# A backward decode kernel bound by its DMA: all loads moved to the stores' ring, zeros in longer rows and smaller portions

## The chip, the cores and the metric

The kernel runs on one core of a Trainium2 chip. The metric is the device time of one execution in microseconds; the time given for a kernel is the median of its executions. A profiled execution also has a span, which is some 2 us shorter (300.1 for 301.83 us before the change). A run is called slow when it lies more than 1.5% above the fastest run of the same kernel; ratios use fast runs alone.

The engines have the profile's names: PE multiplies matrices (PEld loads its weights), ACT and DVE compute and copy, Pool computes masks here, SP only issues transfers. A *ring* is the queue in which the transfers that one engine issued wait for the 16 DMA engines; a transfer *lands* when all of it has arrived. Idle DMA is time in which DMA engines have no packet to move.

## The reference

The reference runs one decode step of an attention layer (4 sequences, 32 query heads, 8 K/V heads, the last 1024 of 4096 cached positions) beside a GeGLU feed-forward layer, and returns the output and all gradients:

```python
q = (xn @ wq).reshape(B, Sq, Hq, Dh)                    # B 4, Sq 1, D 512, Hq 32, Dh 128
k = jnp.repeat(k_cache[:, :, Sk - W:, :], rep, axis=1)  # W 1024 of Sk 4096, rep 4
v = jnp.repeat(v_cache[:, :, Sk - W:, :], rep, axis=1)
p = softmax(einsum("bhqd,bhkd->bhqk", q, k) * Dh ** -0.5)
a = einsum("bhqk,bhkd->bhqd", p, v).reshape(B, Sq, Hq * Dh) @ wo
f = (gelu(xn @ w_gate) * (xn @ w_up)) @ w_down          # F 1792
out = x + a + f                                         # xn = layernorm(x)
_out, _vjp = jax.vjp(_f, x, k_cache, v_cache, wq, wo, w_gate, w_up, w_down)
return (_out, *_vjp(grad_out))
```

The gradients of both caches are full-size, 33.6 MB each. Three quarters of each are zeros, since only 1024 positions take part. Writing 50.3 MB of zeros is the largest single piece of traffic.

## The kernel before

It works in four attention blocks (two K/V heads each) after the feed-forward part. Loads are issued by SP, the stores of computed gradients by Pool, the zeros by ACT: three rings on the same 16 DMA engines. Computed gradients pass through three output buffers (`osb`) and four staging buffers (`stg`).

```python
wres = ctx.enter_context(tc.tile_pool(name="wres", bufs=2))    # wo, wq of two blocks
kvp = ctx.enter_context(tc.tile_pool(name="kvp", bufs=3))      # K and V blocks, 1 MB each
outp = ctx.enter_context(tc.tile_pool(name="outp", bufs=3))    # osb_d, osb_g, osb_o, osb_q
...
def load_kv(t, k, g):
    d_, src, nm = ((k_t, A_k_cache, "kb"), (v_t, A_v_cache, "vb"))[k]
    tl = kvp.tile([P, B, J, Dh], BF16, name=nm, tag=nm)
    nc.sync.dma_start(out=tl[:].rearrange("p b j d -> p b (j d)"), in_=...)
...
ZG = 4                                                         # one transfer: 4 heads, 3.15 MB
def zeros(n):
    zsrc = bass.AP(tensor=ztile.tensor, offset=ztile.offset, ap=[list(ztile[:].ap[0]), [0, ZG], [1, ZW]])
    for _ in range(min(n, len(zlist))):
        og, b, g = zlist.pop(0)
        z = store(nc.scalar, og[b, g:g + ZG, 0:K0, :].rearrange("g (m j) d -> m g (j d)", m=P), zsrc, ...)
        if last_act:                                           # keeps its place in ACT's order
            tc.add_manual_dep(z.ins, last_act[-1].ins.name, NoSync)
...
def scores(t, k):
    for g in range(GP):
        for b in range(B):
            ...
            tick(2)                                            # two pieces of deferred gradient work
            if b == 1 and (g, k) != (0, 0):
                zeros(1)                                       # three per block
...
def piece_o(g, i, held):
    if i == 0:
        held["osb"] = outp.tile([P, rep, D], BF16, name="osb_o", tag="o")
    ...
    if i == rep - 1:
        store(nc.gpsimd, out=out_5[...], in_=held["osb"][:], ...)
...
for t in range(NT):
    scores(t, 0); softmax(t); dvdk(t, 0); scores(t, 1); softmax_d(t); dvdk(t, 1)
    odq(t, 0); pre(t + 1); odq(t, 1); fin(t)
    load_next(t)                                               # K/V of t+1 and t+2, weights of t+2
    dw(t)
tick(len(bg))
zeros(len(zlist))                                              # four transfers are left: 12.6 MB
```

## Time and profile before

| | before |
|---|---|
| time | 302.49 us (301.24 to 303.51, three runs) |
| span of the profile | 300.1 us |
| moved | 112.38 MB, of it 50.46 zeros, 30.81 loads, 30.67 stores |
| end of PE's work | 267 us |
| granted PE clock | 0.83 |

The page's slices, its queue table, the windows and the chain are shown and read in the prediction.

### The profile page before, as it was taken

What the parts mean: (1) busy time and instruction counts of PE and PEld (TensorE: products, weight loads), DVE (VectorE), ACT (ScalarE), POOL (GpSimd) and SP (SyncE); (2) the same over time, 40 slices, a digit from 0 to 9 for tenths busy, and PEclk for the clock granted to TensorE, in tenths of its full rate; (3) what the DMA queues carried; (4) which work ended last, traced back from release to release, by engine and by line L of the source; (5) the groups of instructions that cost most, each with busy time, mean ns of one, the idle gap of its engine ahead of it and who ended that gap; (6) DMA issues with size and microseconds to landing.
All of it is one profiled execution on the core that took longest, in us unless ns stands there. A gap on an engine that the chain in (4) does not pass through costs nothing.

```text
span 300.1 us, 6816 instructions
## 1 busy us (share of the span) xinstructions
PE 206.4 (69%) x2956; PEld 141.9 (47%) x2956; DVE 145.1 (48%) x310; ACT 114.4 (38%) x217; POOL 66.4 (22%) x84
## 2 busy tenths in 40 slices
PE   1397987959779986668997876995759779720000
PEld 0396875636447645435764644673436455320000
DVE  6372763544635673364566445564344537760000
ACT  3002645734425554243565243445235417710000
POOL 6000121622032423103513302251032031400000
PEclk9985999887978897997799789799777968955555
DMA  4999999399999999999999999999699995999997
GB/s 137 381 387 382 379 399 403 131 393 398 400 396 331 381 415 416 419 418 424 410 387 409 423 416 419 419 414 408 260 386 359 392 403 211 340 370 407 418 417 322
DMA packets 34149, 112.38 MB, mean 374 GB/s; under 512 B 1408, under 2 KB 7560, under 8 KB 34120
## 3 DMA queue, kind: packets, MB, share of 16 engines
q10 hardware_dynamic: 8580, 50.46, 41.3%
q1 hardware_dynamic: 17732, 30.81, 28.1%
q0 software_dynamic: 7808, 30.67, 26.2%
q8 instruction: 23, 0.38, 0.5%
q14 instruction: 6, 0.05, 0.0%
HBM read 30.93 MB, written 81.01 MB: 373 GB/s over the span
## 4 chain that ended last, share of the span: by engine, by line
PE 49%; DMA 23%; DVE 11%; ACT 3%; issue 3%; SPq 0%; DVEq 0%; ACTq 0%; POOLq 0%
DMA out_dram<-osb_o 11%; PE T_ps L316 10%; PE kv_ps L424 7%; DMA kb<-in_A_k_cache_dram 6%; PE S_ps L321 4%; DMA wd_sb<-in_B_w_down_dram 4%; DVE T_sb L94 3%; PE wqT_ps L488 3%; DMA out_dram<-osb_d 3%; PE woT_ps L268 3%; PE od_ps L396 2%; PE wgT_ps L636 2%; PE acc_ps L168 2%; PE dwg_ps L609 2%; PE wdT_ps L524 2%
## 5 line engine op out<-in xcount | busy, mean ns | idle before, releaser
L94 DVE COPY T_sb<-T_ps 128x1024 bf16<-128x1024 bf16 x64 | 44.2, 691 | 40.5 <-PE T_ps L316 40.1
L92 ACT CAST stg_dv<-kv_ps 128x512 bf16<-128x512 f32 x52 | 28.9, 588 | 39.9 <-PE kv_ps L424 39.5
L92 ACT CAST stg_dk<-kv_ps 128x512 bf16<-128x512 f32 x46 | 25.0, 588 | 15.1 <-PE kv_ps L424 14.9
L316 PE MATMUL T_ps<-ident,kb 128*128 128x128 bf16 x256 | 24.7, 228 | 5.8 <-DMA kb<-in_A_k_cache_dram 5.3
L316 PE MATMUL T_ps<-ident,vb 128*128 128x128 bf16 x256 | 26.4, 252 | 1.4 <-DVE osb_q L94 1.4
L316 PEld LDWEIGHTS <-kb 128*128 128x128 bf16 x256 | 18.5, 102 | 17.0 <-DMA kb<-in_A_k_cache_dram 5.8
L424 PE MATMUL kv_ps<-domr,P_q 128*128 128x512 bf16 x64 | 24.1, 441 | 0.0
L316 PEld LDWEIGHTS <-vb 128*128 128x128 bf16 x256 | 20.2, 114 | 7.6 <-issue 3.7
L92 ACT CAST osb_q<-dwq_ps 128x512 bf16<-128x512 f32 x25 | 13.6, 589 | 21.1 <-DMA out_dram<-osb_o 11.2
L424 PE MATMUL kv_ps<-qmr,dS_q 128*128 128x512 bf16 x64 | 20.8, 410 | 0.6 <-ACT stg_dv L92 0.3
L92 ACT CAST osb_g<-dwg_ps 128x384 bf16<-128x384 f32 (+1 forms) x30 | 14.5, 534 | 13.5 <-PE dwg_ps L609 7.8
L94 DVE COPY woT<-woT_ps 128x1024 bf16<-128x1024 bf16 x16 | 11.1, 692 | 16.1 <-PE woT_ps L268 16.1
L92 ACT CAST osb_o<-dwo_ps 128x512 bf16<-128x512 f32 x23 | 12.9, 587 | 11.5 <-PE dwo_ps L443 10.9
L332 POOL TENSOR_TENSOR dS_q<-dS_b,qmsk 128x1024 bf16<-128x1024 bf16 x4 | 7.5, 1884 | 33.3 <-DVE dS_b L385 33.3
L458 PE MATMUL dwq_ps<-od_r,xnm 128*128 128x256 bf16 x64 | 12.5, 320 | 2.5 <-DVE osb_q L94 2.3
L321 PE MATMUL S_ps<-T_sb,dom 128*32 128x256 bf16 x128 | 10.2, 307 | 5.2 <-DVE T_sb L94 5.2
L94 DVE COPY wqT<-wqT_ps 128x1024 bf16<-128x1024 bf16 x16 | 11.0, 689 | 5.6 <-PE wqT_ps L488 5.4
L488 PEld LDWEIGHTS <-wq_sb 128*128 128x128 bf16 x128 | 11.1, 121 | 5.1 <-issue 4.1
L488 PE MATMUL wqT_ps<-ident,wq_sb 128*128 128x128 bf16 x128 | 13.0, 260 | 0.0
L94 DVE CAST stg_dk<-kv_ps 128x512 bf16<-128x512 f32 x18 | 12.1, 686 | 1.4 <-PE kv_ps L424 1.3
L268 PE MATMUL woT_ps<-ident,wo_sb 128*128 128x128 bf16 x128 | 12.3, 240 | 0.5 <-DVE dST L94 0.3
L98 POOL DMA_DIRECT2D out_dram<-stg_dv x8 | 6.2, 775 | 28.5 <-ACT stg_dv L92 22.8
(187 smaller groups left out, 365.1 us busy)
## 6 DMA issues: line engine op xcount, KB each, us to landing
out_dram<-ztile ACTq DMA_DIRECT2D x16, 3072.0 KB, 16.3
kb<-in_A_k_cache_dram SPq DMA_DIRECT2D x8, 1024.0 KB, 17.4
vb<-in_A_v_cache_dram SPq DMA_DIRECT2D x8, 1024.0 KB, 21.2
out_dram<-stg_dv POOLq DMA_DIRECT2D x8, 1024.0 KB, 10.2
out_dram<-stg_dk POOLq DMA_DIRECT2D x8, 1024.0 KB, 9.4
wo_sb<-in_A_wo_dram SPq DMA_DIRECT2D x4, 1024.0 KB, 17.0
wq_sb<-in_A_wq_dram SPq DMA_DIRECT2D x4, 1024.0 KB, 18.1
out_dram<-osb_o POOLq DMA_DIRECT2D x8, 512.0 KB, 11.8
```

The lines of the kernel that those rows point to most:

```text
L92: last_act.append(nc.scalar.copy(out=out, in_=in_))
L94: return nc.vector.tensor_copy(out=out, in_=in_)
L98: d = eng.dma_start(out=out, in_=in_)
L168: nc.tensor.matmul(ps[:, c, :], lhsT=lf(c), rhs=rhs, start=(k == 0), stop=(k == len(terms) - 1))
L268: nc.tensor.transpose(wT_ps[:, i, c, :], wo_sb[:, 2 * h2 + i, c * P:(c + 1) * P], ident[:])
L316: nc.tensor.transpose(T_ps[:, j, :], blks[(t, g)][:, b, j, :], ident[:])
L321: nc.tensor.matmul(ps[q * RG:(q + 1) * RG, :], lhsT=lf[:, s * RG:(s + 1) * RG], rhs=T_sb[:, q * WQ:(q + 1) * WQ], start=(g == 0 and b == 0 ...
L332: nc.gpsimd.tensor_tensor(out=dst[:], in0=src[:].unsqueeze(1).broadcast_to([P, NQ, WQ]), in1=qmsk[:].unsqueeze(2).broadcast_to([P, NQ, WQ] ...
L396: nc.tensor.matmul(od_ps[b * RB:b * RB + rep, k, g, :], lhsT=pT[:, jj, c0:c0 + rep], rhs=blks[(t, g)][:, b, j, :], start=(j == 0), stop=(j ...
L424: nc.tensor.matmul(mps[:].rearrange("p b d -> p (b d)"), lhsT=src[:, q, jj * P:(jj + 1) * P], rhs=mr[:, g].rearrange("p b d -> p (b d)"), ...
L458: nc.tensor.matmul(mps[:, i].rearrange("p g d -> p (g d)"), lhsT=xnm[:, i2 * 2 + i, c * P:(c + 1) * P], rhs=dq_r[:].rearrange("p g d -> p ...
L488: nc.tensor.transpose(wT_ps[:, i, c, :], wq_sb[:, c, h * Dh:(h + 1) * Dh], ident[:])
```

## The change

The intent: in the kernel before, Pool's ring (software in the queue table) sends its stores in packets of 3.9 KB on average where SP's sends loads in packets of 1.74 KB, so loads should cost less engine time on Pool's ring; longer zero rows should cost less too (the prediction's estimate: 462 ns for 12 KB, where two packets of 6 KB take 470); and zeros spread in small portions over all compute steps should fill the DMA's idle stretches. To make room for the 12 KB zero tile, the second set of `wo` and `wq` gets a pool that is opened only after the feed-forward part, so its load can no longer be issued at the start.

```diff
-    wres = ctx.enter_context(tc.tile_pool(name="wres", bufs=2))
+    wres = ctx.enter_context(tc.tile_pool(name="wres", bufs=1))      # odd blocks: a second pool, later
...
-        nc.sync.dma_start(out=wd_sb[:], in_=...)                     # likewise wg, wu, wo, wq, kb, vb
+    nc.gpsimd.dma_start(out=wd_sb[:], in_=...)                       # and moved to the top of the kernel
...
-    ZW = K0 // P * Dh
+    ZP = P // 2
+    ZW = K0 // ZP * Dh                                               # rows of 12 KB on 64 partitions
...
-    ZG = 4
-            z = store(nc.scalar, ...m=P), zsrc, "zeros", ["rest", "zeros"])
-            if last_act: ... NoSync
+    ZG = 2                                                           # 1.57 MB
+        zs = ztile[0:P:P // ZP, :]
+            z = store(nc.sync, ...m=ZP), zsrc, "zeros", ["rest"])
+            tc.add_manual_dep(z.ins, after.ins.name, SYNC)           # after the newest copy out of PSUM
...
+    def step():
+        tick(2)
+        steps[0] += 1
+        if steps[0] % ZEVERY == 0:                                   # ZEVERY = 4
+            zeros(1, last[-1])
...
-                tick(2)                                              # in pre, scores and fin
-                if b == 1 and (g, k) != (0, 0):
-                    zeros(1)
+                step()
+            if f2 == NF // 2 - 1: zeros(1, last[-1])                     # two more, in the feed-forward part
```

## The prediction

> **What bounds the kernel now.** I first read the page's slices, then its queue table, to see whether anything is full for most of the span.
>
> ```profile
> PE   1397987959779986668997876995759779720000
> DMA  4999999399999999999999999999699995999997
> GB/s 137 381 387 382 379 399 403 131 393 398 400 396 331 381 415 416 419 418 424 410 387 409 423 416 419 419 414 408 260 386 359 392 403 211 340 370 407 418 417 322
> ```
>
> The DMA row is 9 almost everywhere, while PE ends four slices (30 us) before the end. So the kernel moves its 112.38 MB about as fast as the 16 DMA engines go, and the last 30 us are transfer alone. The queue table has who moves what; q10 is ACT's ring (zeros), q1 SP's (loads), q0 Pool's (stores):
>
> ```profile
> q10 hardware_dynamic: 8580, 50.46, 41.3%
> q1 hardware_dynamic: 17732, 30.81, 28.1%
> q0 software_dynamic: 7808, 30.67, 26.2%
> ```
>
> The shares sum to 95.6%. Bytes over time: zeros 50.46 MB in 0.413 x 300.1 = 123.9 us, that is 407 GB/s; loads 30.81 MB in 84.3 us, 365 GB/s; stores 30.67 MB in 78.6 us, 390 GB/s. Bytes over packets: 5.9, 1.74 and 3.9 KB. Small packets are the dear ones. Next, the windows, to find where the engines are *not* full (the last two columns are DMA share and GB/s):
>
> ```profile
> 0.00:7.50 7.50, 0.80 (x5) 0.44 (x5) 4.59 (x23) 2.86 (x3) 4.74 (x24) 1.00 0.44 137
> 52.50:60.00 7.50, 7.49 (x84) 4.97 (x81) 3.86 (x8) 5.41 (x13) 4.80 (x4) 0.85 0.32 126
> 208.00:216.00 8.00, 3.90 (x32) 2.23 (x33) 1.79 (x3) 0.78 (x2) 0.75 (x1) 0.79 0.78 314
> 246.00:255.00 9.00, 8.58 (x75) 4.98 (x74) 6.21 (x11) 6.35 (x12) 0.89 (x2) 0.81 0.64 239
> 270.00:300.00 30.00, 0.00 (x0) 0.00 (x0) 0.64 (x1) 0.00 (x0) 0.00 (x0) 0.50 0.96 393
> ```
>
> One minus share, times length: 4.2, 5.1, 1.8, 3.2 and 1.2 us idle. With 0.7, 0.8 and 0.6 us from the windows 216 to 225, 225 to 232 and 255 to 262 it is 17.6 us in all. Last, the chain in order of time (start, length, what), for what compute waits for:
>
> ```profile
> 1.59 10.67 DMA wd_sb<-in_B_w_down_dram
> ...
> 109.66 13.90 DMA out_dram<-osb_o
> ...
> 161.07 13.91 DMA out_dram<-osb_o
> ...
> 194.70 17.36 DMA kb<-in_A_k_cache_dram
> ...
> 259.83 4.48 DMA out_dram<-osb_o
> ```
>
> Compute itself is paced by transfers: it waits for an output buffer's store to land, or for a K block. I therefore treat the time as bytes over rate, plus idle DMA, not as a sum of engine work.
>
> [...] q0 averages 3.9 KB although most of its rows are 1 or 2 KB, while SP's loads go out as single rows of 1, 2 and 3.5 KB. I counted the packet records between 118 and 133 us, when all three rings have work: Pool, SP and ACT move 127, 66 and 222 GB/s, near the ratio of their packets (4, 2 and 6 KB). [...] the best slice here has 424. [...] Pool's stores take 0.54 to 0.92 us to issue, all along.
>
> **The change, part by part.**
>
> *Loads in 4 KB packets.* Median packet times in the records are 46 ns (1 KB), 84 (2 KB), 144 (3.5 KB), 159 (4 KB) and 235 (6 KB): about 8 ns plus 37.8 ns per KB. SP has 6024 packets of 1 KB, 10240 of 2 KB and 1024 of 3.5 KB: (277 + 860 + 147) / 16 = 80.3 us. As 7522 packets of 4 KB they are 74.7 us. Saved: 5.6 us of full engine time.
>
> *Zeros in 12 KB rows.* 8192 x 235 ns / 16 = 120.3 us. 4096 rows at 8 + 12 x 37.8 = 462 ns are 118.3 us. Saved: 2.0 us. Together 7.6 us, about 2.5%.
>
> *When zeros are released.* Before: 16 DMAs of 3.15 MB, the first at 59.5 us, three per attention block, four (12.6 MB, 30 us at 417 GB/s) after compute. After: 32 of 1.57 MB. There are 96 compute steps (4 first, then 16 in scores, 4 in fin, and 4 in the next pre, per block), so 24 zeros there, 2 in the feed-forward part, and 6 (9.4 MB, 22.6 us) at the end. The two early ones, and one per four steps from then on, fill most of the 5.1 us hole at 52.5 us. The tail shrinks by 7.5 us; this is not a second gain, as the bytes go into holes or delay something else.
>
> *The path, stage by stage.* The last K block lands at 212 us. Summing the windows, 80.6 MB moved by then, in 212 - 10.8 idle = 201 us, 401 GB/s. After, the zeros released by that point are 21 x 1.57 = 33.0 MB rather than 28.3, so some 85 MB must pass; the rate gains 6.9 of 201 us (all of the loads, two thirds of the zeros), to 415 GB/s: 205 us, plus some 5.5 us idle (start 3.7, rest of the hole 1, elsewhere 1) is 210.5. From that landing to the end of compute is 55 us before (212 to 267), the only stretch where compute is visibly the limit; some osb waits shorten without SP's loads, I take 53. Then 22.6 us of zeros and 0.9 us for the last stores. Sum: 210.5 + 53 + 23.5 = 287 us. A timed run before is 302.49 with a span of 300.1; I add 1.5 us rather than 2.4, since the profiled run itself took 301.83: 288.5, rounded to 288.
>
> *What moves without a gain.* Zero issues leave ACT's queue, where one blocked ACT 5.6 us, but at 267.7 us, when compute is done. The two weight buffers now come from two pools; the second set is asked for after the feed-forward part (about 45 us) and first used near 85, so it stays hidden. The first load is issued from Pool near 0.8 us instead of SP at 1.59: perhaps 1 to 2 us earlier for wd_sb.
>
> **Rivals.**
>
> *Head of line on Pool.* In the built kernel, Pool's queue has K, V and weight loads between the stores, each with waits on PE, and each DMA also waits for the one eight places earlier to land. Around the end of block 0 six transfers of 1 MB stand ahead of the osb_o stores on which the chain above waits, so those waits may grow from 14 to 20 us. For it: FIFO order, and Pool also computes the masked tiles. Against it: a stalled compute releases no zeros, so the ring then gets all 16 engines; the bytes still flow. If it costs 4 us in each of three blocks as idle DMA: about 300, the same.
>
> *Zeros crowd out the ring.* By the packet ratio seen, 12 KB against 4 KB gives zeros three quarters while they are pending. Against it: 1.57 MB at three quarters of 418 GB/s is 5 us in each 8 us of four steps, and no zero is pending in the rest. It delays loads by some us; about 293.
>
> *Idle in the last block instead.* No loads are left there: 8.4 MB of stores and 5 zeros (7.9 MB) in 53 us are 16.3 MB, or 40 us at 410. If idle there grows from 7 to 13 us, and the earlier stages gain nothing more, the gain is the 7.6 us of packets alone: about 294.
>
> *Rate better than fitted.* If full stretches rise to 425 GB/s throughout, 112.4 MB take 264.5 us; with 15 us idle: 281.
>
> **Range and chances.** 288 us, with 8 in 10 between 279 and 297. Faster by over 2% means under 296.4: only head of line at its full cost, or two rivals together, prevent it. Chances: faster 0.82, within 2% 0.14, slower 0.04.
>
> **What would show it.** Packets fall from 34149 to about 20,000, nearly all of 4 KB or more; loads move at over 395 GB/s in the first 35 us (now 381 to 384); the slice near 55 us is full; the gap between PE's end and the span's end is about 23 us instead of 30; the last K block lands near 210. Wrong would be: new long waits of Pool for DMA landings, DMA digits under 9 in blocks 1 and 2, a zero packet well above 470 ns[...], or Pool issues of several us[...].

## More of the kernel before

The waits view of the kernel before shows what engines wait for, as a sum in us, the number of waits and the longest. These lines, out of many, name DMAs:

```profile
ACT osb_q L92 <- DMA out_dram<-osb_o: 11.2, 3, 4.3
...
PEld L316 <- DMA kb<-in_A_k_cache_dram: 5.8, 1, 5.8
```

The first means that ACT could not write a gradient into an output buffer before the store that last used it had landed. The waits are there, but none is longer than 6 us.

## The result

The changed kernel takes 318.63 us (315.66 to 320.24, four runs), the kernel before 302.98 us on the same chip (301.24 to 303.51, four runs). The ratio is 1.052 (95% interval 1.043 to 1.061): slower. A ratio here is the mean of one kernel's fast runs over the mean of the other's fast runs of the same rounds, so it is not quite the ratio of the medians. Both profiled runs are fast: spans 317.1 and 300.1 us, granted clock 0.81 and 0.83. The lower clock is not the cause: PE is busy for 205.4 us, and for 206.4 before.

The slices and queues of the changed kernel's page answer to those that the prediction shows (q0 is Pool's ring, now with loads and stores; q1 is SP's, now with the zeros):

```profile
PE   1478957708699860758789586688895888952000
DMA  4999997997679999997999999989999987499997
GB/s 152 389 379 384 385 409 280 305 378 288 287 287 348 341 424 413 379 412 309 312 388 398 394 414 412 382 297 406 354 380 423 394 336 283 194 351 356 410 439 303
DMA packets 20261, 112.38 MB, mean 354 GB/s; under 512 B 1664, under 2 KB 1928, under 8 KB 16136
...
q0 software_dynamic: 15344, 61.35, 52.7%
q1 hardware_dynamic: 4756, 50.47, 38.5%
```

The packets are as intended (34149 before). But the rate of the early slices, where nothing but loads moves, is 379 to 389 GB/s, and was 379 to 387 before; a slice is 7.9 us long, and the DMA row falls below 9 from 71 to 95 us and again from 254 to 277 us; PE has two slices at 0, from 63 to 71 and from 119 to 127 us, which it did not have before. Now the windows, for two stretches of the first block. In the last two columns stand DMA share and GB/s. First the kernel before:

```profile
60.00:80.00 20.00, 16.10 (x200) 10.02 (x199) 10.04 (x19) 8.54 (x19) 4.10 (x5) 0.83 0.99 396
80.00:100.00 20.00, 16.82 (x263) 11.52 (x261) 10.39 (x25) 8.31 (x17) 7.11 (x5) 0.83 1.02 372
```

Then the changed one:

```profile
60.00:80.00 20.00, 9.70 (x84) 5.71 (x84) 5.65 (x10) 5.50 (x12) 5.82 (x6) 0.74 0.84 336
80.00:100.00 20.00, 16.62 (x231) 11.23 (x234) 11.72 (x25) 9.68 (x20) 7.14 (x7) 0.91 0.76 309
```

In the first stretch PE stands still for half the time *and* the DMA is not full, but not at the same moment. Cut at 70 us, the changed kernel has

```profile
60.00:70.00 10.00, 2.50 (x28) 1.37 (x28) 1.38 (x2) 0.27 (x1) 4.19 (x3) 0.81 0.99 392
70.00:100.00 30.00, 23.82 (x287) 15.57 (x290) 15.99 (x32) 14.90 (x31) 8.76 (x10) 0.84 0.73 299
```

While PE waits, the DMA works off what is queued; it falls idle when PE runs again. In the second stretch, compute runs nearly as before, and the DMA is at three quarters. The chain in order of time names the stops (start, length, what):

```profile
53.01 17.56 DMA out_dram<-osb_g
...
104.40 23.37 DMA kb<-in_A_k_cache_dram
...
163.64 17.27 DMA kb<-in_A_k_cache_dram
...
189.44 15.98 DMA out_dram<-osb_o
...
223.87 11.27 DMA kb<-in_A_k_cache_dram
...
238.97 13.51 DMA out_dram<-osb_o
```

And the waits view has the same as time lost by the engines:

```profile
PEld L340 <- DMA kb<-in_A_k_cache_dram: 17.6, 3, 11.8
ACT osb_q L92 <- DMA out_dram<-osb_o: 16.9, 4, 6.9
...
ACT osb_g L92 <- DMA out_dram<-osb_g: 10.4, 1, 10.4
```

A 0.46 MB store that takes 17.56 us to land is not slow in itself: an osb_g store of this kernel with nothing ahead of it landed 2.8 us after its issue (87.17 us). The one of 53.01 us was issued behind two weight loads of 1 MB each (51.33 and 52.25 us) in the same ring, and landed 1.1 us after the second of them (70.57 and 69.49 us).

**Two sums that the rest of this document uses.** From the trace's packet records I counted how many packets are in flight on the 16 engines at each moment; what is missing to 16 is idle DMA, summed over the span. What remains of the span is full DMA time. Before: 19.1 us idle, 281.0 full. After: 29.6 idle, 287.5 full. So the 17 us of span are 10.5 us more idle and 6.5 us more full time. Full time should have shrunk: if each packet took the median that its size has in the kernel before (462 ns for the 12 KB ones), the changed kernel would need 7.4 us less (268.2 against 275.6 us of all engines; 7.6 were predicted). But the time beyond these medians rose from 10.4 to 20.7 us, which more than eats it up. A part of this is that the median of a 4 KB packet is 165 ns in the changed kernel, and 159 before.

### The profile page after: what moved, and what is told of

Its sections match the earlier page's. It is cut to its first block, busy times and chain, and to the rows that moved or that the text cites. A ratio compares the mean times of both kernels' runs of the same rounds, so it can differ in the third digit from the quotient of the medians.

```text
span 317.1 us, 6847 instructions
## 1 busy us (share of the span) xinstructions
PE 205.4 (65%) x2940; PEld 142.6 (45%) x2956; DVE 147.9 (47%) x310; ACT 113.8 (36%) x217; POOL 88.8 (28%) x111
## 4 chain that ended last, share of the span: by engine, by line
DMA 38%; PE 24%; issue 16%; DVE 7%; POOL 4%; ACT 3%; DVEq 0%; ACTq 0%; POOLq 0%
DMA kb<-in_A_k_cache_dram 16%; DMA out_dram<-osb_o 12%; PE T_ps L340 7%; DMA out_dram<-osb_g 6%; DMA wo_sb<-in_A_wo_dram 5%; PE kv_ps L446 4%; PE S_ps L345 3%; POOL out_dram L99 1%; PE dwg_ps L623 1%; DVE T_sb L94 1%; ACT stg_dk L92 1%; PE woT_ps L292 1%; PE wqT_ps L510 1%; PE od_ps L418 1%; PE dwq_ps L480 1%
## 5 line engine op out<-in xcount | busy, mean ns | idle before, releaser
L340 PE MATMUL T_ps<-ident,kb 128*128 128x128 bf16 x256 | 26.9, 243 | 25.4 <-DMA kb<-in_A_k_cache_dram 16.3
L92 ACT CAST stg_dv<-kv_ps 128x512 bf16<-128x512 f32 x52 | 28.6, 588 | 26.1 <-PE kv_ps L446 25.4
L340 PEld LDWEIGHTS <-kb 128*128 128x128 bf16 x256 | 20.1, 109 | 36.2 <-DMA kb<-in_A_k_cache_dram 17.6
L340 PE MATMUL T_ps<-ident,vb 128*128 128x128 bf16 x256 | 27.8, 251 | 2.8 <-ACT osb_q L92 2.6
L340 PEld LDWEIGHTS <-vb 128*128 128x128 bf16 x256 | 21.0, 114 | 11.0 <-issue 5.9
L92 ACT CAST osb_g<-dwg_ps 128x384 bf16<-128x384 f32 (+1 forms) x30 | 14.4, 535 | 20.8 <-DMA out_dram<-osb_g 10.4
L92 ACT CAST osb_o<-dwo_ps 128x512 bf16<-128x512 f32 x23 | 12.8, 588 | 24.6 <-PE dwo_ps L465 23.6
L446 PE MATMUL kv_ps<-domr,P_q 128*128 128x512 bf16 x59 | 20.7, 430 | 0.7 <-DVE osb_q L94 0.6
L446 PE MATMUL kv_ps<-qmr,dS_q 128*128 128x512 bf16 x59 | 19.1, 400 | 1.1 <-ACT stg_dv L92 0.3
L94 DVE COPY woT<-woT_ps 128x1024 bf16<-128x1024 bf16 x16 | 11.1, 692 | 14.4 <-PE woT_ps L292 14.4
L99 POOL DMA_DIRECT2D out_dram<-osb_o x8 | 6.3, 793 | 30.7 <-ACT osb_o L92 17.7
L99 POOL DMA_DIRECT2D out_dram<-osb_q x8 | 5.9, 731 | 31.4 <-ACT osb_q L92 26.7
L292 PEld LDWEIGHTS <-wo_sb 128*128 128x128 bf16 x128 | 9.9, 110 | 8.9 <-issue 7.3
L510 PEld LDWEIGHTS <-wq_sb 128*128 128x128 bf16 x128 | 11.1, 121 | 5.1 <-issue 3.9
L99 POOL DMA_DIRECT2D out_dram<-stg_dk x8 | 6.2, 771 | 24.2 <-ACT stg_dk L92 19.8
## 6 DMA issues: line engine op xcount, KB each, us to landing
out_dram<-stg_dk POOLq DMA_DIRECT2D x8, 1024.0 KB, 16.8
wo_sb<-in_A_wo_dram POOLq DMA_DIRECT2D x4, 1024.0 KB, 17.6
```

The lines of the kernel that those rows point to most:

```text
L92: last.append(nc.scalar.copy(out=out, in_=in_))
L94: last.append(nc.vector.tensor_copy(out=out, in_=in_))
L99: d = eng.dma_start(out=out, in_=in_)
L292: nc.tensor.transpose(wT_ps[:, i, c, :], wo_sb[:, 2 * h2 + i, c * P:(c + 1) * P], ident[:])
L340: nc.tensor.transpose(T_ps[:, j, :], blks[(t, g)][:, b, j, :], ident[:])
L446: nc.tensor.matmul(mps[:].rearrange("p b d -> p (b d)"), lhsT=src[:, q, jj * P:(jj + 1) * P], rhs=mr[:, g].rearrange("p b d -> p (b d)"), ...
```

## The experiments

All kernels gave correct results. Two theories stood at the outset. *The ring*: Pool's ring serves in order, so small stores and K blocks wait behind bulk transfers, and engines wait for them. *The release*: one small transfer of zeros (a portion) per four compute steps, and never a stock of them, leaves the DMA idle where compute is the bound, and takes engine time where K blocks are. "Before" ran on the same chip each time (300.95 to 301.92 us median).

### First set: parts alone

**The loads on Pool, nothing else.**

```diff
 # the kernel before
-        nc.sync.dma_start(...)      # all weight, K and V loads
+        nc.gpsimd.dma_start(...)
```

> The kernel before with one part of the change: all loads from Pool's queue, zeros as they were (6 KB rows, 3.15 MB each, from ACT). Theory 1 (one in-order ring: K blocks and small stores wait behind bulk loads): slower than before by 8 to 18 us, 310 to 320, with K blocks landing over 20 us after their issue and waits on osb stores longer than the 14 us of before. Theory 2 (it is the zeros: 12 KB packets taking three quarters, or their release by steps): 299 to 305, as before.

Measured: 318.26 us, ratio 1.056 (1.047 to 1.065). The loads on Pool alone cost as much as the whole change. The chain between 30 and 66 us of this run:

```profile
35.78 18.61 DMA out_dram<-osb_d
```

and of the kernel before, where the same kind of store is waited for:

```profile
40.74 8.04 DMA out_dram<-osb_d
```

One shortcoming: the loads stand after the mask set-up in Pool's program and start at 6.0 us, 4.4 us late; the change hoists them. The first weights landed 2.9 us later, so up to 3 of the 16 us are of that.

**The change with its loads back on SP.** The zeros then go to ACT's queue.

```diff
 # the changed kernel
-    nc.gpsimd.dma_start(...)        # all loads
+    nc.sync.dma_start(...)
-            z = store(nc.sync, ...)
+            z = store(nc.scalar, ...)     # NoSync, as before
```

> The changed kernel with the loads back on SP; zeros stay 12 KB rows, one per four steps and two early, but issued from ACT in its program order[...]. Theory 1: the loss goes and the early zeros gain: 286 to 297. Theory 2: still slow, 310 to 320.

Measured: 314.68 us, ratio 1.045 (1.039 to 1.051). The run is flawed: with the hoisted loads on SP, the load of `grad_out` came to stand behind 5.5 MB of weights, and the feed-forward part began 6 to 7 us late. It was mended below.

**The size of the zero rows.**

```diff
 # the changed kernel
-    ZP = P // 2
+    ZP = P                          # 6 KB rows on all partitions
```

> The changed kernel with the zeros as 6 KB rows from all 128 partitions, same bytes and same release. Theory 1: no change beyond 2%, 314 to 321. Theory 2 in its form of packet turns (12 KB against 4 KB): Pool's share beside zeros rises from a quarter to 40%, loads and stores land sooner, 303 to 311.

Measured: 315.4 us, ratio 1.049 (1.043 to 1.056). That is 3 us less than the changed kernel, with overlapping intervals: no gain of 12 KB rows is to be seen. 12 KB rows in the kernel before were not run.

**The output stores off Pool's ring, in the changed kernel.**

```diff
 # the changed kernel
-                store(nc.gpsimd, out=...)   # osb_d, osb_g, osb_o, osb_q
+                store(nc.scalar, out=...)
```

> The changed kernel with only the small stores (osb buffers, 0.25 to 0.5 MB) issued from ACT, so that they do not stand behind loads in Pool's ring; K, V, weights and the stg stores stay there. Theory 1, if the store waits make most of the loss: 303 to 311, landing of osb stores under 9 us. Theory 1, if the K block waits (23, 20 and 11 us) make most: 312 to 318. Theory 2: 316 to 320.

Measured: 320.6 us, ratio 1.068 (1.061 to 1.075). Compute ended 9.4 us earlier, but in SP's order three transfers of zeros stuck until 252.5 us, the DMA idled (34.8 us in all), and 36.4 us of transfers followed the last osb_q store in place of 26.2. The expected help at the start did not come either; the chain there has

```profile
41.21 18.48 DMA out_dram<-osb_d
```

so a ring of its own did not free the store.

### Second set: the ring, the release

**The output stores on SP, loads on Pool, all else as before.**

```diff
 # the kernel before with all loads on Pool
-                store(nc.gpsimd, out=...)   # osb_d, osb_g, osb_o, osb_q
+                store(nc.sync, out=...)
-    ctx.enter_context(tc.manual_schedule(engines={nc.sync.engine}))   # SP's order is left to the scheduler
```

> The kernel before with all loads on Pool's ring (that alone cost +16 us) and the small output stores moved off Pool's ring to SP's. If the loss of that earlier run was the small stores waiting behind bulk loads in one in-order ring, the waits for osb and stg_d buffers fall from 17-25 us to under 10 us, and the time comes back to 300-306 us. If the loss was in the loads themselves on Pool's ring (later start, slower K blocks), it stays at 312-318 us.

Measured: 312.5 us, ratio 1.036 (1.029 to 1.043), so 6 of 16 us came back. The waits for output buffers did not fall as expected (sum 21.1 and 17.0 us for osb_q). The store at the start still took

```profile
40.51 13.93 DMA out_dram<-osb_d
```

The packet sizes fit this. SP's ring sends osb rows of 1 KB as packets of 1 KB, Pool's ring sends loads as 4 KB. Counted over these 13.9 us, SP's ring moves 116 GB/s (1587 packets, 1.0 KB each) and Pool's 282 (952 packets, 4.1 KB each). In the kernel before it was the reverse, stores in 4 KB against loads of 1 and 2 KB: over the 8.0 us, the stores' ring moves 162 GB/s and the loads' 239. So this experiment exchanged a place at the back of a line for a smaller share. The lower share is shown; that it makes all of the store's slowness is not.

**The change with loads on SP, mended.**

```diff
 # the second experiment of the first set
-    for eng, dst, src in ((nc.sync, dy_b, grad_out), (nc.scalar, x_b, A_x)):
+    for eng, dst, src in ((nc.scalar, dy_b, grad_out), (nc.scalar, x_b, A_x)):
```

> The changed kernel with loads on SP, zeros in 12 KB rows on ACT's queue, and grad_out loaded on ACT's queue so that it no longer stands behind the first weights. If the new release of the zeros (one per four compute steps, no stock of them, six left for the end) costs time by itself, this is still slower than before: 306-311 us. If what the version of this without the moved grad_out load lost (+13 us) was all that late load and the later start it gave, it is 300-303 us.

Measured: 308.68 us, ratio 1.019 (1.008 to 1.029). Two of the four runs count as slow, and whether it is slower than before by more than 2% is unclear. Taking the loads off Pool's ring (the zeros then go to ACT's) brings the changed kernel down by 10 us; some 7 us stay with the release and the layout.

**The release alone.**

```diff
 # the kernel before
-    ZG = 4
+    ZG = 2
-                if b == 1 and (g, k) != (0, 0):
-                    zeros(1)
+                step()              # one zero per four steps; also in pre and fin
```

> The kernel before with one thing changed: the zeros are halved to 1.57 MB each and released one per four compute steps of every kind, on ACT's queue, without those before the first block. If the release costs time by itself (DMA idle where the compute is the bound, K blocks shared with zeros where the loads are), 306-311 us with DMA idle 5-10 us above that of before. If only the amount of bytes counts and not when they go, 300-303 us.

Measured: 311.31 us, ratio 1.027 (1.018 to 1.036), again with two slow runs of four and unclear as to 2%; idle 26.7 us, 7.6 more than before, as expected. The slices of this run (7.6 us each) have the idle DMA from 61 to 99 us and from 229 to 260 us:

```profile
DMA  4999999983787999999999999999997856999997
```

The first of these holes is the one that the changed kernel has too. From 70 to 100 us, the mended experiment above (loads on SP) has

```profile
70.00:100.00 30.00, 22.83 (x319) 14.64 (x319) 15.01 (x31) 12.13 (x25) 6.20 (x6) 0.77 0.67 260
```

and the kernel with the loads on Pool and nothing else

```profile
70.00:100.00 30.00, 22.57 (x311) 14.04 (x310) 13.91 (x30) 11.41 (x23) 9.68 (x11) 0.83 1.00 389
```

So this hole goes with the release and not with the ring.

**More zeros among the steps, in the changed kernel.**

```diff
 # the changed kernel
-    ZEVERY = 4
+    ZEVERY = 3
```

> The changed kernel with one zero per three compute steps in place of four, so that all 32 go out among the steps and none is left for the end. If idle DMA for want of released zeros is a main part of the loss, DMA idle falls from 30 to about 22 us and the time to 306-311 us. If the ring's order is what holds the loads and stores, the time stays at 315-319 us: the zeros only crowd the K blocks sooner.

Measured: 319.82 us, ratio 1.064 (1.059 to 1.069). The tail was gone (7.3 us from the last osb_q store to the end), but compute was stretched by as much. The waits view has

```profile
PEld L340 <- DMA kb<-in_A_k_cache_dram: 36.0, 3, 15.6
```

twice as much as in the changed kernel: with loads on Pool, zeros sent earlier are paid for by K blocks, and idle rose to 33.5 us all the same. The release theory, as a cure for the changed kernel, missed here.

### Third set: take away what makes the engines wait

**Six output buffers in the changed kernel.** (The room comes from 6 KB zero rows.)

```diff
 # the changed kernel, ZP = P
-    outp = ctx.enter_context(tc.tile_pool(name="outp", bufs=3))
+    outp = ctx.enter_context(tc.tile_pool(name="outp", bufs=6))
```

> The changed kernel with six output buffers in place of three (zeros as 6 KB rows to make room, which by itself changed at most 3 us). If what loads on Pool's ring cost is paid where a fourth store waits for the landing of the first in the same ring, the waits of 10.4 us (osb_g) and 16.9 us (osb_q) in the changed kernel nearly vanish, and the time falls to 303-309 us. If the cost is in the K blocks that wait in that ring or in the DMA's own amount of time, it stays at 313-318 us, with K waits at least as long as before.

Measured: 305.1 us median, ratio of the fast runs 1.002 (0.995 to 1.009). The four runs spread from 301.7 to 315.2 us, and the profiled one (307.5 us) counts as slow. Over the 315.4 us of the same kernel with three buffers the gain is 10 us by the medians and 13 by the fast runs, but one run of the four (315.17) shows none. The waits of osb_q for osb_o are no longer among the larger ones, while K waits stay where they were:

```profile
PEld L340 <- DMA kb<-in_A_k_cache_dram: 19.5, 3, 9.6
```

A store still took 26.61 us to land in the chain (issued at 45.77 us): the ring is as slow as ever, but it stops fewer engines. The DMA is idle for 0.8 us from 70 to 100 us, in place of 8.1.

**More zeros in the first and last block of the kernel before.**

```diff
 # the kernel before
-                if b == 1 and (g, k) != (0, 0):
+                if b == 1 and ((g, k) != (0, 0) or t in (0, NT - 1)):
```

> The kernel before with one more 3.15 MB zero transfer in the first block and one more in the last (four in place of three there), nothing else. If the DMA was idle there for want of released zeros (5 us near 52 us, 8 us after 200 us), the end comes 6-10 us sooner: 292-296 us. If the added zeros only crowd the loads and stores, it is 299-304 us.

Measured: six runs from 292.32 to 303.65 us, median 302.09. One run shows the hoped-for gain, one (298.09) about half of it, four show none. With three output buffers the gain is not to be relied on.

**Both together, loads on SP.** The changed kernel's layout, loads on SP, `grad_out` on ACT's queue, six output buffers, zeros of 3.15 MB in 6 KB rows on ACT's queue as before, with the two added transfers.

```diff
 # the mended experiment above
-    outp = ... bufs=3    ZP = P // 2    ZG = 2
+    outp = ... bufs=6    ZP = P         ZG = 4
-        if steps[0] % ZEVERY == 0: zeros(1, last[-1])
+                if b == 1 and ((g, k) != (0, 0) or t in (0, NT - 1)): zeros(1, last[-1])
```

> A candidate: the changed kernel's memory layout (that frees room for six output buffers), but loads on SP, zeros of 3.15 MB in 6 KB rows on ACT's queue as before with one more in the first and the last block, and no zeros before the first block. If the ring and the release of the zeros are the two costs of the change, this is at or under the kernel before with the same release: 288-296 us. If the layout itself (one set of weights less held ahead) costs, 300-308 us.

Measured: 289.68 us, ratio 0.959 (0.953 to 0.964): faster than both (one run of four, 298.84, counts as slow). The two early portions of the feed-forward part are gone here as well. The DMA row of its page is the reason:

```profile
DMA  7999998999999999999999999999999999999995
```

Only 7.2 us of the span are idle.

### Fourth set: what the gain and the loss are of

**The same without the two added zero transfers.**

```diff
-                if b == 1 and ((g, k) != (0, 0) or t in (0, NT - 1)):
+                if b == 1 and (g, k) != (0, 0):
```

> The candidate that took 290 us, without its two added zero transfers: six output buffers and the changed memory layout, loads on SP, and the release of the zeros exactly as in the kernel before. If the gain of the candidate came from the output buffers, this stays at 288-292 us; if it came from the two added zero transfers, it is 298-303 us; in between it is both.

Measured: 301.28 us, ratio 0.991 (0.982 to 1.000), near the kernel before; two runs of four count as slow. Compute ended 3 us earlier than there (PE at 263.7 against 267.0 us), but from the last osb_q store to the end are 37.6 us in place of 33.8, which takes the gain back. By the medians, buffers (with the layout) alone and zeros alone gain next to nothing; together they gain 12 us.

**The 290 us kernel with its loads on Pool.**

```diff
-    nc.sync.dma_start(...)          # all loads
+    nc.gpsimd.dma_start(...)
```

> The 290 us candidate with its loads moved to Pool's ring, zeros left as they are. With six output buffers a store that waits behind loads no longer stops an engine. If the whole cost of the shared ring was the wait of the output buffers, this is within 4 us of the candidate: 288-294 us. If the K blocks that queue behind stores in the ring cost by themselves, it is 297-305 us.

Measured: 311.6 us, ratio 1.031 (1.025 to 1.037). The ring costs 22 us even with six buffers, where at most 4 were expected had it been a matter of output buffers only. Of these, 6.9 us are lost before the first block: `x_b`, 128 KB on ACT's queue, landed 5 us later (at 17.9 us in place of 12.6). In the last block another 16.4 us are lost to a K block. The chain of this run has

```profile
209.54 27.45 DMA kb<-in_A_k_cache_dram
```

where that of the 290 us kernel has

```profile
199.00 14.18 DMA kb<-in_A_k_cache_dram
```

When it was issued, one V load, two osb_q stores, two stg_dv stores and an osb_o store were in the ring ahead of it and had not landed.

**The change's release with six buffers, loads on SP.**

```diff
 # the mended experiment above
-    outp = ... bufs=3    ZP = P // 2
+    outp = ... bufs=6    ZP = P
```

> The changed kernel's release of the zeros (1.57 MB, one per four compute steps) with six output buffers and loads on SP, zeros of 6 KB rows on ACT's queue. Against the candidate (290 us) it tells what the release costs when stores stop nothing: if the release costs 6-8 us as it did with three buffers, 296-299 us; if that cost too was paid through output buffers, 289-292 us. Against the run of the changed kernel with six buffers and loads on Pool's ring (about 302-305 us) it tells the ring apart a second time.

Measured: 299.95 us, ratio 0.991 (0.985 to 0.998). That is a little above what was expected, 10 us slower than the kernel with lumps (the transfers of 3.15 MB) and two more of them, and no slower than the one with the lumps as before.

### The runs side by side

Times are medians of all runs. Idle and full are counted over the packet records of the profiled run (in the two runs marked *, that run counts as slow); a recount agrees to within 0.2 us.

| loads | release of zeros | osb buffers | time | idle | full |
|---|---|---|---|---|---|
| SP | lumps (before) | 3 | 301.9 | 19.1 | 281.0 |
| SP | one per four steps, release alone | 3 | 311.3 | 26.7 | 278.9 |
| SP | one per four steps, mended | 3 | 308.7 | 25.4 | 281.3 |
| Pool | lumps | 3 | 318.3 | 31.7 | 285.1 |
| Pool | lumps, osb stores on SP | 3 | 312.5 | 28.6 | 282.7 |
| Pool | one per four steps (after) | 3 | 318.6 | 29.6 | 287.5 |
| Pool | one per three steps | 3 | 319.8 | 33.5 | 284.5 |
| Pool | one per four steps | 6 | 305.1* | 20.6 | 285.0 |
| Pool | lumps and two more | 6 | 311.6 | 25.9 | 284.8 |
| SP | lumps | 6 | 301.3* | 16.8 | 283.1 |
| SP | one per four steps | 6 | 300.0 | 16.5 | 281.0 |
| SP | lumps and two more | 6 | 289.7 | 7.2 | 280.8 |

Full time lies between 279 and 287 us in all of them; idle time runs from 7 to 34 us and largely sets the order. In the three pairs that differ by the ring (the lines 1 and 4, 3 and 6, 12 and 9 of the table), loads on Pool raise full time by 4 to 6 us and idle by 4 to 19. And the costs don't add: loads on Pool cost 16 to 17 us with the old release and 10 with the new; the new release costs 7 to 9 us with loads on SP and nothing more with loads on Pool. A likely reading is that both end in the same thing, an engine stopped on a landing, and that one stop hides behind the other; no run tests it.

## Why the prediction was wrong

The prediction put 288 us and a chance of 0.04 on slower. It had split the time at the landing of the last K block. That is where the error lies: the block landed at 235.1 us (223.87 + 11.27 in the chain) and not at 210.5. From there to the end of PE's work were 56.5 us for a predicted 53, and 25.5 us of end for 23.5. So 24.6 of the 30 us of error are in the first term, "to 415 GB/s: 205 us, plus some 5.5 us idle": it was 216.0 us of full time and 19.1 idle. It is the ring that moves this landing. With the same release and the loads on SP (the mended experiment) the block landed at 215.5 us, with the loads on Pool and nothing else changed at 228.8, with the release alone at 213.1, and before at 212.1. So 19.6 of the 24.6 us go with the ring (10 of them last to the end: the mended experiment needs 66.4 us from the landing to the end of PE's work, in place of 56.5). Three steps of the prediction failed: the gain from larger load packets, which did not come; the rival *Head of line on Pool*, turned down because the bytes would flow on; and the early zeros, which were to leave almost no idle DMA.

- **"Loads in 4 KB packets. Saved: 5.6 us of full engine time."** The packets came as predicted, but no time was saved. From 14 to 34 us, when only loads move, the kernel before has this line in the windows view:

```profile
14.00:34.00 20.00, 17.64 (x392) 15.93 (x391) 11.96 (x36) 4.29 (x8) 0.72 (x1) 0.74 1.05 386
```

 and the changed kernel this:

```profile
14.00:34.00 20.00, 16.04 (x377) 14.38 (x377) 10.99 (x34) 3.73 (x8) 2.25 (x4) 0.74 1.02 385
```

The rate is the same; the share sank from 1.05 to 1.02. The prediction had read the 159 ns of a 4 KB packet from the kernel before, where only *stores* have that size. For the loads of this stretch the median is 173 ns (1319 packets). At 173 ns the prediction's 7522 packets are 81.3 us, no less than the 80.3 of the small ones. A share over 1 also says that records of packets overlap (up to 21 are in flight at once on the 16 engines), so that packet times divided by 16 are more than the time that passes. Why a load's packet takes longer there is open. The sign that it had named itself, "over 395 GB/s in the first 35 us", did not appear.

- **"The rate gains 6.9 of 201 us, to 415 GB/s."** By the last K block 83.6 MB had moved (85 predicted), in 235.1 less 19.1 us of idle: 387 GB/s, below the 401 of before. Besides the missing gain, there are stretches of 4 to 8 us in which the slowest tenth of the 4 KB packets takes over 310 ns, in one over 510 (165 is their median), mostly where loads start again while no packet of zeros starts (near 56, 104, 154, 212 and 228 us). In the three pairs that differ by the ring, the time above the medians of the kernel before rose from 10.4 to 17.3 us, from 11.8 to 20.7 and from 10.6 to 17.1. That it goes with Pool's ring is shown; by what cause is open.

- **"Some 5.5 us idle" up to that point.** There were 19.1 us: 4.3 at the start (3.7 predicted), 2.3 from 45 to 60 us, 8.1 from 70 to 100 and 4.4 later. The 8.1 go with the release: with loads on SP, the mended experiment and the release alone idle for 10.1 us in the same stretch, and with loads on Pool and the old release it is 0.5.

- **The rival *Head of line on Pool*.** The prediction had seen it, sized it at 12 us and turned it down with "a stalled compute releases no zeros, so the ring then gets all 16 engines; the bytes still flow". One ring alone does fill the engines (a share of 1.02 from 14 to 34 us, when only Pool's loads move), and the bytes do flow while something is queued. The store of 53.01 us stops ACT for 10.4 us, and from 60 to 70 us the DMA is not idle at all; but what is queued is being used up, and what follows then comes in the small portions above. Where the lumps are kept (loads on Pool, nothing else), the idle time comes at once: a store that took 18.61 us to land holds compute and with it the first zeros (68.91 us in place of 59.53), and from 52 to 70 us 11.1 us are idle in place of 5.2. The order in the ring is in the traces: all 44 transfers of Pool's ring before the change and all 71 after it landed in the order of their issue, the store of 53.01 us 1.1 us behind the loads ahead of it. The wait for the transfer eight places earlier is seen too: none of Pool's transfers was issued before that one had landed, and the loads of 16.84 and 21.38 us followed it by 0.3 us. Six buffers, which take most of the stores' waits away, brought 10 to 13 us, and taking the loads out of the ring 10 us. So the direction of this rival is shown by two experiments, and its size was underestimated. That it was so because the zeros are released by the compute that the ring stops is what these stretches suggest; no run separates it.

- **K blocks.** The prediction looked at osb stores only. K blocks in the ring wait behind stores as well: 17.6 us of PE waits in the changed kernel (5.8 before), and 16.4 us of one stage in the Pool version of the 290 us kernel. Pool's own program could also have issued these loads late, since it holds stores and masks; but in the changed kernel the K loads of 163.64 and 223.87 us were issued within 0.3 us of the last reads of their buffer, so the time was lost after the issue.

- **"Early zeros fill the hole at 52.5 us."** Half right. The share of that window went from 0.32 to 1.00 (at 306 GB/s), but the hole moved on to 70 to 100 us (8.1 us idle). The portions were too small and too rare to stand in for a stock: between 78 and 98 us 4.1 MB of zeros went out, with the stores 6.0 MB, where 20 us of the engines at 410 GB/s are 8 MB.

- **The end.** Right as to the change. From the last osb_q store to the end are 33.8 us before and 26.2 after, 7.6 less for a predicted 7.5. The level was 2 us too low: the prediction reckoned 30 us after PE's end before and 23.5 after, but its own 267 of 300.1 us leave 33.1, and less 7.5 that is the 25.6 that came (25.5). The prediction had also been right that this is no gain by itself: what left the end was paid for earlier. With one zero per three steps the end shrank to 7.3 us and the kernel was no faster.

- **Zeros in 12 KB rows.** The packet took its predicted 462 ns, and the rate shows no loss from the use of 64 partitions, every other one. In the end stretch the windows view has 417 GB/s for the kernel before (275 to 295 us) and for the changed kernel

```profile
296.00:312.00 16.00, 0.00 (x0) 0.00 (x0) 0.00 (x0) 0.00 (x0) 0.00 (x0) 0.50 1.02 426
```

The gain is 2% on 9.4 MB, half a microsecond; 6 KB rows in the changed kernel were, if anything, 3 us faster.

- **The signs of being wrong.** DMA digits under 9 appeared, as named. Long waits *of Pool* for landings did not: it was ACT and PE that waited, since it was their buffers. Pool's issues took 0.54 to 1.24 us each, with a median of 0.75 as before.

What stays open: the cause of the slow packets, 6.5 to 9 us in the three pairs; how much of a store's slowness in a ring of its own is its smaller packets; and why buffers and the two added zero transfers gain 12 us only together (the table shows the idle time that vanishes, not which wait it was).

## What to carry to other kernels

Before putting transfers of different urgency in one ring, list what will stand ahead of each transfer that an engine waits for: in this kernel, with the loads on Pool's ring, the osb_d store at the start took 18.6 us to land in place of 8.0, and in the changed kernel the waits for K blocks were 17.6 us in place of 5.8. Where fill-in traffic is released by compute, count idle DMA and waiting engines together, stage by stage: with the loads alone on Pool, the first zeros came 9.4 us later behind the stopped compute, and 11.1 us of DMA were idle from 52 to 70 us in place of 5.2. In this kernel a stock of fill-in work was worth 7 to 9 us more than an even spread with three output buffers, and nothing with six. A packet time read from stores did not hold for loads here (159 ns, and 173 where only loads move), and packets times packet time was not the time that passed (shares of 1.05 and 1.02 from 14 to 34 us): look at the rate of a stretch in which only these packets move.
